# Decode block (attention times gated unit): x for the last sum by VectorE copies, and Wo's rows 0 to 30 in six pieces

## The chip, the cores and the metric

The kernel runs on one core of one Trainium2 chip, as one launch. The metric is the device time in microseconds (us). A core has a matrix engine (PE; its weight loads are listed as PEld), VectorE (DVE), ScalarE (ACT), GpSimd (POOL), SyncE (SP, which here only issues DMAs) and 16 DMA engines that move data between HBM and the on-chip memory, SBUF. Each engine works through its own list of instructions in order, and an instruction waits on semaphores for what it needs.

## The reference, cut to what matters

```
x = A_x                                  # 8 x 1 x 512, bfloat16
xn = layernorm(x)
q = xn @ wq                              # 32 heads of 128
k, v = last 2048 positions of the caches # 8 kv heads, 4 q heads share one
p = softmax(q k^T * 128 ** -0.5)
s = (p v) @ wo                           # 4096 x 512
b = (sigmoid(xn @ w_gate) * (xn @ w_up)) @ w_down
out = x + s * silu(b)
```

Everything is bfloat16 in memory. The change touches two of these terms only: the `x` of the last sum, and how `wo` gets into SBUF.

## The kernel before, in words

All large data comes through a ring of five SBUF buffers of 4 MB each (`ring_tile`). Every load is issued by SP, on one DMA queue, in a fixed order (`loads`): Wq, K of the batch rows 0 to 2, V of row 0, then K and V in turn to the last row, then w_gate and w_up (one buffer), w_down, and Wo. `issue_loads` hands out a load whenever `free_bufs` says that a buffer has come free. K and V take 4 MB for each of the 8 batch rows, 64 MB of the 81 MB that the kernel reads.

At the start VectorE computes the layer norm from `x_bf` (the loaded x), PE transposes it, and VectorE then builds a number of small constants from an identity matrix (lines 212 to 287) while POOL makes others (masks, zero fills). Those constants are used from the first softmax on. The query is projected when Wq has landed.

The loop over `b` (line 614) does, for each batch row, the turning of K on VectorE (`k_turn`, four pieces), the scores on PE (`qk`), the softmax, and the product with V of earlier rows (`pv`, `pv_rows`). The result of all rows is gathered in `o2_sb`.

After the loop come the gated unit (`unit_in`, `unit_mid`, `unit_out`, which leaves silu(b) in `gate`) and the product with Wo. `load_wo` brings the 32 row blocks of Wo (a block is 128 KB, one row `m` for each of the 128 partitions) in five DMAs for the blocks 0 to 30, then block 31 in two halves of 64 KB. `out_row(m, s)` multiplies block `m`: four matmuls for the two halves `s` and the two column parts `c`. A block's matmuls wait for the DMA that brought it. The sum over `m` of half 0 is complete, and is multiplied by `gate` into `prod` (line 690), when the first half of block 31 has gone through; the second half follows the same way. Then line 694 adds x:

```
nc.vector.tensor_tensor(out=y_bf[:], in0=prod[:], in1=x2_sb[:], op=ALU.add)
```

and SP and ACT each store one half of the columns (line 696).

In this layout column part 0 lies on the partitions 0 to 7 and part 1 on 32 to 39. So x is wanted once more, in `x2_sb`, with its first 256 columns on partitions 0 to 7 and the other 256 on 32 to 39. `x2_sb` is cleared by POOL at the start (line 94). `load_x2` fills it: POOL copies the first half from `x_bf` (line 122), and SP issues a 4 KB DMA for the second half (line 123). That load stands in the list right after V of row 1 and takes no ring buffer.

The DMAs use eight completion semaphores in turn. Before a DMA is issued, SP waits until the one that used the same semaphore last has landed. At the end of the kernel this means that each half of Wo's block 31 (line 153) is issued only when an earlier load (w_gate for the first, w_up for the second) is there.

Of the kernel before, what the change touches and what calls it, by code (L numbers as in the profile page):

```python
# [10 lines left out]
def kernel(  # L11
# [13 lines left out]
    nc = tc.nc  # L25
    P = 128
    B, _, D = A_x.shape
# [22 lines left out]
    NCOL = 2  # L50
    DC = D // NCOL
# [31 lines left out]
    x_bf = work.tile([B, D], bf16, name="x_bf")  # L83
    nc.scalar.dma_start(out=x_bf[:], in_=A_x.flatten_outer_dims())

    def ring_tile(name):
        return ring.tile([P, BIG], bf16, name=name, tag="ring", align_bytes=ALIGN)
# [5 lines left out]
    x2_sb = work.tile([NCOL * 32, DC], bf16, name="x2_sb")  # L93
# [24 lines left out]
        v_tiles[b] = t  # L118
        load_heads(t, A_v_cache, b)

    def load_x2():
        nc.gpsimd.tensor_copy(out=x2_sb[:B, :], in_=x_bf[:, :DC])
        nc.sync.dma_start(
            out=x2_sb[32 : 32 + B, :], in_=A_x.flatten_outer_dims()[:, DC:]
        )

    def load_in():
        t = ring_tile("wgu_sb")
        for n, w in enumerate((B_w_gate, B_w_up)):
            v = t[:, n * KT * F : (n + 1) * KT * F].rearrange(  # L130
                "p (kt n) -> p kt n", kt=KT
            )
            nc.sync.dma_start(out=v, in_=w.rearrange("(p kt) n -> p kt n", kt=KT))
            w_tiles["gu"[n]] = v
# [7 lines left out]
    def load_wo():  # L142
        t = ring_tile("wo_sb")
        v = t[:].rearrange("p (m n) -> p m n", m=MR)
        src = A_wo.rearrange("(p m) n -> p m n", m=MR)
        for m0, m1 in ((0, 11), (11, 19), (19, 25), (25, 29), (29, 31)):
            nc.sync.dma_start(out=v[:, m0:m1, :], in_=src[:, m0:m1, :])  # L147
        last, last_src = (
            w[:, MR - 1, :].rearrange("p (c s n) -> p s c n", c=NCOL, s=2)
            for w in (v, src)  # L150
        )
        for s in range(2):
            nc.sync.dma_start(out=last[:, s], in_=last_src[:, s])
        w_tiles["o"] = v

    loads = [(load_wq,), (load_k, 0), (load_k, 1), (load_k, 2), (load_v, 0)]
    for b in range(3, B):
        loads += [(load_k, b), (load_v, b - 2)]
        if b == 3:
            loads.append((load_x2,))  # L160
    loads += [(load_v, B - 2), (load_v, B - 1), (load_in,), (load_down,), (load_wo,)]
    free_bufs = [RING]

    def issue_loads():
        while loads:
            small_one = loads[0][0] is load_x2
            if not small_one and free_bufs[0] == 0:
                return
            f, *a = loads.pop(0)
            f(*a)  # L170
            if not small_one:
                free_bufs[0] -= 1

    issue_loads()


# [14 lines left out]
        out=rstd[:], in_=mv[:, 1:2], func=AF.Sqrt, bias=eps_t[:], scale=1.0  # L191
# [4 lines left out]
        out=xn_bf[:],  # L196
# [7 lines left out]
    for kt in range(KT):  # L204
        nc.tensor.transpose(
            out=xnT_ps[:, kt, :], in_=xn_bf[:B, kt::KT], identity=ident[:B, :B]
        )
    xnT_sb = work.tile([P, KT, PW], bf16, name="xnT_sb")
    nc.vector.memzero(xnT_sb[:])
    nc.vector.tensor_copy(out=xnT_sb[:, :, :B], in_=xnT_ps[:])  # L210

    rows16 = consts.tile([P, GR], f32, name="rows16")
    nc.vector.tensor_reduce(
        out=rows16[:],
        in_=ident[:].rearrange("p (g x) -> p x g", x=GR),
# [4 lines left out]
    for gg in range(NG):  # L220
# [3 lines left out]
            out=t[:, :, gg],  # L224
            in_=rows16[:]
# [8 lines left out]
        out=quarter[:],  # L234
        in_=ident[:].rearrange("p (h q) -> p q h", q=QP),
# [4 lines left out]
        out=block[:], in_=quarter[:].unsqueeze(2).to_broadcast([P, QP, PW])  # L240
# [3 lines left out]
        out=same[:],  # L244
        in_=ident[:].rearrange("p (g j r) -> p g r j", j=QP, r=rep),
# [5 lines left out]
        out=SumM[:].rearrange("p (g j r) -> p g j r", j=QP, r=rep),  # L251
        in_=same[:]
# [6 lines left out]
        out=Jneg[:],  # L259
        in_=ident[:].rearrange("p (a j r) -> p j a r", j=QP, r=rep),  # L260
# [4 lines left out]
        out=Jneg[:], in0=Jneg[:], scalar1=-scale, scalar2=None, op0=ALU.mult  # L265
# [3 lines left out]
        out=Hm[:],  # L269
        in_=ident[:].rearrange("p (a gl) -> p gl a", gl=GL),  # L270
# [5 lines left out]
        out=Cm4[:],  # L276
        in_=ident[:].rearrange("p (u c x) -> p c u x", c=4, x=GR),
# [5 lines left out]
        out=Cm2[:],  # L283
        in_=ident[:].rearrange("p (u c x) -> p c u x", c=2, x=GR),
# [5 lines left out]
        out=heads[:], in_=same[:].unsqueeze(2).to_broadcast([P, XR, QP])  # L290
# [3 lines left out]
        out=spr[:],  # L294
        in_=ident[:].rearrange("k (gl cl p) -> k cl p gl", gl=GL, cl=CL),
    )
    quad = consts.tile([P, QP, QP, PW], bf16, name="quad")
    for a in range(QP):
        nc.gpsimd.tensor_copy(
            out=quad[:, :, a, :], in_=ident[:].rearrange("k (a w) -> k a w", a=QP)  # L300
# [10 lines left out]
    for s in range(2):  # L311
# [13 lines left out]
        for e in range(2):  # L325
            nc.vector.tensor_copy(  # L326
                out=qx_sb[:, s, :, :, e, :],
                in_=q_ps[:].rearrange(
                    "p (r wb w e) -> p e r wb w", r=rep, wb=WE // 2, e=2
                )[:, e],  # L330
            )
    free_bufs[0] += 1
    issue_loads()
    qT_sb = work.tile([P, 2 * rep * WE, PW], bf16, name="qT_sb")
    nc.vector.transpose(
        out=qT_sb[:].rearrange("p m b -> p (m b)"),
        in_=qx_sb[:].rearrange("p s r wb e w -> p (s r wb e w)"),
    )
    qc_sb = work.tile([P, GL, NG, rep, WE, B], bf16, name="qc_sb")
    for i in range(2):  # L340
        qr_ps = psum.tile([P, 2, 2 * rep * WE * B], f32, name="qr_ps", tag="o_ps")
        for aa in range(2):
# [9 lines left out]
            out=qc_sb[:, 2 * i : 2 * i + 2].rearrange("p gl g r we b -> p (gl g r we b)"),  # L352
            in_=qr_ps[:].rearrange("p a m -> p (a m)"),
# [260 lines left out]
    for b in range(B + 1):  # L614
# [25 lines left out]
        if turn:  # L640
            qk(b)
            free_bufs[0] += 1
            issue_loads()
            if s - 1 >= 0:
                for gg in range(NG):
                    pv(s - 1, gg)
        else:
            pv(s - 1, 1)
# [37 lines left out]
    for m in range(MR):  # L686
        for s, n in enumerate(halves):
            out_row(m, s)
            if m == MR - 1:
                nc.vector.tensor_tensor(  # L690
                    out=prod[:, n], in0=gate[:, n], in1=a_ps[s][:], op=ALU.mult
# [3 lines left out]
    for c in range(NCOL):  # L695
        queues[c].dma_start(
            out=out.flatten_outer_dims()[:, DC * c : DC * (c + 1)],
            in_=y_bf[32 * c : 32 * c + B, :],
# [31 lines left out]
```

## Time and profile before

| What | Value |
|---|---|
| median of 3 runs | 197.61 us (197.59 to 197.65) |
| profiled execution | 197.44 us, of which the profile's span is 195.7 us |
| outside the span | 1.74 us |
| mean granted PE clock | 0.81 |
| busy: PE, DVE, ACT, POOL | 57%, 60%, 20%, 3% of the span |
| DMA queue of SP | 6368 packets, 81.01 MB, 97.2% of 16 engines' span |
| HBM read | 414 GB/s over the span |
| POOL copy into x2_sb (line 122) | 0.39 us, at 11.12 us |
| issue of the x DMA (line 123) | at 38.7 us |
| matmuls with Wo (line 676) | 128, busy 4.6 us, from 185.9 us |

All times in the profile are us from the start of the span. In the timeline a line gives the start, the time from the first to the last of a group, the engine, the source line, the operation, and in brackets the idle time before it with what ended it. In the chain of work that ended last, each line gives start, duration and what the end was waiting for. In the table by stretches, a column gives an engine's busy time with its number of instructions, and the last three are the granted PE clock, the mean busy share of the 16 DMA engines and GB/s. The profile lists the tile `x2_sb` as `x_sb` and `o2_sb` as `o_sb`.

### The profile page before, as it was taken

The numbers are of one execution on the slowest core, as the hardware profiler recorded it, in microseconds if no ns is written. First come the engines' busy times: TensorE is split into PE (matmuls) and PEld (weight loads), VectorE is DVE, ScalarE is ACT, GpSimd is POOL, SyncE is SP. The second block draws the span as 40 slices with busy tenths as digits, with TensorE's granted clock in tenths as the row PEclk, the third lists the DMA queues.
The fourth block names the chain that finished last, engine by engine and source line by source line (L and its number), as shares of the span: only waits on it lengthen the run. The fifth ranks groups of instructions, "written<-read, shape, count | busy, mean of one in ns | idle before, by whom it ended". The sixth has DMA issues, their size and how long they took to land.

```text
span 195.7 us, 2620 instructions
## 1 busy us (share of the span) xinstructions
PE 111.6 (57%) x1092; PEld 44.6 (23%) x1092; DVE 117.6 (60%) x176; ACT 38.6 (20%) x112; POOL 6.4 (3%) x22
## 2 busy tenths in 40 slices
PE   0133025709809980799059914990796199684362
PEld 0011001102002240214022411150215024462351
DVE  3404498299299449935895489739936952455001
ACT  3001910015015011501141104211501110233000
POOL 2730000000000000000000000000000000000000
PEclk9999555966985996589757985699589669999998
DMA  6999999999999999999999999999999999999991
GB/s 241 457 408 442 432 429 429 429 432 425 429 429 429 427 429 429 432 424 439 432 439 422 439 435 435 429 432 425 432 429 429 425 429 429 429 431 429 416 396 41
DMA packets 6410, 81.17 MB, mean 415 GB/s; under 512 B 992, under 2 KB 1024, under 8 KB 1408
## 3 DMA queue, kind: packets, MB, share of 16 engines
q1 hardware_dynamic: 6368, 81.01, 97.2%
q8 instruction: 8, 0.13, 0.2%
q10 hardware_dynamic: 32, 0.01, 0.0%
q14 instruction: 2, 0.02, 0.0%
HBM read 81.01 MB, written 0.01 MB: 414 GB/s over the span
## 4 chain that ended last, share of the span: by engine, by line
PE 38%; DVE 35%; DMA 23%; ACT 1%; issue 1%; SPq 1%; DVEq 0%
PE s_ps L401 27%; DVE k_sb L384 27%; DMA wo_sb<-in_A_wo_dram 12%; DMA k_sb<-in_A_k_cache_dram 11%; PE o_ps L501 8%; DVE pt_bf L441 2%; DVE o_r L522 2%; PE o_ps L530 1%; DVE o_sb L552 1%; ACT o_r L518 1%; DVE o_q L543 1%; DVE mx L414 1%; PE a_ps L676 1%; SPq L147 0%; SPq L101 0%
## 5 line engine op out<-in xcount | busy, mean ns | idle before, releaser
L384 DVE STREAM_TRANSPOSE k_sb<-k_sb 128x2048 uint32<-128x2048 uint32 x32 | 72.9, 2291 | 5.7 <-DMA k_sb<-in_A_k_cache_dram 5.7
L401 PE MATMUL s_ps<-k_sb,qz 128*32 128x512 bf16 x256 | 61.6, 1086 | 11.8 <-DVE k_sb L384 11.5
L447 PE MATMUL pc_ps<-pt_bf,spr 128*32 128x128 bf16 x128 | 4.7, 292 | 40.7 <-DVE pt_bf L441 40.7
L414 DVE TENSOR_REDUCE mx<-s_ps 128x1 f32<-128x512 f32 x8 | 5.5, 691 | 29.0 <-PE s_ps L401 29.0
L501 PE MATMUL o_ps<-v_sb,pT_sb 128*32 128x256 bf16 (+1 forms) x416 | 21.0, 298 | 0.0
L401 PEld LDWEIGHTS <-qz 128*32 128x32 bf16 x256 | 8.8, 115 | 49.8 <-issue 49.7
L501 PEld LDWEIGHTS <-pT_sb 128*32 128x32 bf16 (+1 forms) x416 | 14.0, 101 | 14.5 <-issue 9.9
L362 ACT COPY qz<-qc_sb 32x64 bf16<-32x64 bf16 x64 | 16.4, 302 | 0.7
L518 ACT ACTIVATE o_r<-o_ps,Cm 128x128 f32<-128x128 f32 x16 | 5.9, 368 | 52.0 <-PE o_ps L501 52.0
L522 DVE SCALAR_TENSOR_TENSOR o_r<-o_ps,Cm,o_r 128x128 f32<-128x128 f32 x28 | 9.7, 350 | 9.8 <-ACT o_r L518 9.3
L428 ACT ACTIVATE p_bf<-s_ps,nm 128x512 bf16<-128x512 f32 x8 | 5.5, 687 | 49.7 <-DVE nm L425 49.7
L447 PEld LDWEIGHTS <-spr 128*32 128x32 bf16 x128 | 3.4, 121 | 41.4 <-issue 40.7
L530 PE MATMUL o_ps<-o_r,rows 128*128 128x128 f32 x32 | 7.5, 320 | 4.8 <-DVE o_r L522 4.8
L483 DVE TENSOR_SCALAR pT_sb<-pc_bf,Hm 128x512 bf16<-128x512 bf16 x32 | 9.0, 352 | 0.2 <-ACT pc_bf L457 0.2
L457 ACT CAST pc_bf<-pc_ps 128x512 bf16<-128x512 f32 x8 | 4.7, 586 | 20.3 <-PE pc_ps L447 20.3
L316 PE MATMUL q_ps<-wq_sb,xnT_sb 128*32 128x512 bf16 x32 | 3.8, 626 | 6.8 <-DMA wq_sb<-in_A_wq_dram 6.5
L676 PE MATMUL a_ps<-wo_sb,o_sb 128*32 128x128 bf16 x128 | 4.6, 219 | 3.9 <-DMA wo_sb<-in_A_wo_dram 3.9
L530 PEld LDWEIGHTS o_ps<-o_r,rows 128*128 128x128 f32 x32 | 4.8, 189 | 6.7 <-DVE o_r L522 6.7
L326 DVE CAST qx_sb<-q_ps 128x256 bf16<-128x256 f32 x4 | 1.5, 420 | 7.7 <-PE q_ps L316 7.7
L441 DVE STREAM_TRANSPOSE pt_bf<-p_bf 128x512 bf16<-128x512 bf16 x8 | 5.4, 675 | 0.9 <-ACT p_bf L428 0.9
L543 DVE SCALAR_TENSOR_TENSOR o_q<-o_ps,rden,block 128x128 f32<-128x128 f32 x8 | 2.8, 351 | 4.7 <-PE o_ps L530 4.7
L690 DVE TENSOR_TENSOR prod<-gate,a_ps 64x128 bf16<-64x128 f32 x2 | 0.5, 279 | 7.5 <-PE a_ps L676 7.5
(64 smaller groups left out, 56.2 us busy)
## 6 DMA issues: line engine op xcount, KB each, us to landing
k_sb<-in_A_k_cache_dram SPq DMA_DIRECT2D x8, 4096.0 KB, 29.9
v_sb<-in_A_v_cache_dram SPq DMA_DIRECT2D x8, 4096.0 KB, 23.4
wq_sb<-in_A_wq_dram SPq DMA_DIRECT2D x1, 3072.0 KB, 11.6
wgu_sb<-in_B_w_gate_dram SPq DMA_DIRECT2D x1, 1792.0 KB, 25.1
wgu_sb<-in_B_w_up_dram SPq DMA_DIRECT2D x1, 1792.0 KB, 28.9
wd_sb<-in_B_w_down_dram SPq DMA_DIRECT2D x1, 1792.0 KB
wo_sb<-in_A_wo_dram SPq DMA_DIRECT2D x1, 1408.0 KB
wq_sb<-in_A_wq_dram SPq DMA_DIRECT2D x1, 1024.0 KB
```

The source lines that it names most:

```text
L362: nc.scalar.copy(out=z[rows, GL * gg : GL * (gg + 1), :, c0 : c0 + rep], in_=qc_sb[rows, :, gg, :, :, b].rearrange("p gl r we -> p gl we r"),)
L384: nc.vector.transpose(out=words, in_=words)
L401: nc.tensor.matmul(s_tiles[b][PW * gl : PW * (gl + 1), :], lhsT=qz[b % 2][:, h, we, :], rhs=kv[:, gg, gl, we // 2, we % 2], start=(we == 0 ...
L414: nc.vector.reduce_max(out=mx[:], in_=s_tiles[b][:], axis=AX.X)
L441: nc.vector.transpose(out=pt_bf[:].rearrange("p c g a r -> p (c g a r)"), in_=p_bf[:])
L447: nc.tensor.matmul(pc_ps[PW * a : PW * (a + 1), cl], lhsT=spr[:, cl].rearrange("k p gl -> k (p gl)"), rhs=pt_bf[:, :, :, a, :], start=True ...
L483: nc.vector.tensor_scalar(out=pT[:, :, :, gl, :], in0=pc[:].rearrange("p c g r -> p g c r"), scalar1=Hm[:, gl : gl + 1], scalar2=None, op0 ...
L501: nc.tensor.matmul(o_ps[rows * cg : rows * (cg + 1), :], lhsT=pT_tiles[b][:, gg, nch * m : nch * (m + 1)].rearrange("p c g r -> p (c g r)" ...
L518: nc.scalar.activation(out=o_r[:], in_=o_ps[:, 0:Dh], func=AF.Copy, scale=cm[:, 0:1])
L522: nc.vector.scalar_tensor_tensor(out=o_r[:], in0=o_ps[:, Dh * c : Dh * (c + 1)], scalar=cm[:, c : c + 1], in1=o_r[:], op0=ALU.mult, op1=AL ...
L530: nc.tensor.matmul(o2_ps[:], lhsT=rows128[gg][:].rearrange("p gl g r q -> p (gl g r q)"), rhs=o_r[:], start=(gg == 0), stop=(gg == NG - 1),)
L676: nc.tensor.matmul(a_ps[s][32 * c : 32 * (c + 1), :], lhsT=o2_sb[:, m, :], rhs=w_tiles["o"][:, m, DC * c + HC * s : DC * c + HC * (s + 1)] ...
```

## The change

The x for the last sum is no longer loaded a second time. `load_x2` is gone, with its POOL copy, its DMA and the exception for it in `issue_loads`. Instead VectorE makes two copies from `x_bf` into `x2_sb`, right after it has written the transposed layer norm (`xnT_sb`) and before it builds the constants. Blocks 0 to 30 of Wo come in six DMAs, of 7, 7, 6, 5, 4 and 2 blocks, where there were five, of 11, 8, 6, 4 and 2. The two halves of block 31 are as before.

```diff
-    def load_x2():
-        nc.gpsimd.tensor_copy(out=x2_sb[:B, :], in_=x_bf[:, :DC])
-        nc.sync.dma_start(
-            out=x2_sb[32 : 32 + B, :], in_=A_x.flatten_outer_dims()[:, DC:]
-        )
-
...
-        for m0, m1 in ((0, 11), (11, 19), (19, 25), (25, 29), (29, 31)):
+        for m0, m1 in ((0, 7), (7, 14), (14, 20), (20, 25), (25, 29), (29, 31)):
             nc.sync.dma_start(out=v[:, m0:m1, :], in_=src[:, m0:m1, :])
...
-        if b == 3:
-            loads.append((load_x2,))
...
     def issue_loads():
-        while loads:
-            small_one = loads[0][0] is load_x2
-            if not small_one and free_bufs[0] == 0:
-                return
+        while loads and free_bufs[0]:
             f, *a = loads.pop(0)
             f(*a)
-            if not small_one:
-                free_bufs[0] -= 1
+            free_bufs[0] -= 1
...
     nc.vector.tensor_copy(out=xnT_sb[:, :, :B], in_=xnT_ps[:])
+
+    for c in range(NCOL):
+        nc.vector.tensor_copy(
+            out=x2_sb[32 * c : 32 * c + B, :], in_=x_bf[:, DC * c : DC * (c + 1)]
+        )
```

## The prediction

> **What bounds the kernel now.** I read the page first, for which resource is full:
>
> ```profile
> DMA  6999999999999999999999999999999999999991
> q1 hardware_dynamic: 6368, 81.01, 97.2%
> q8 instruction: 8, 0.13, 0.2%
> ```
>
> The 16 DMA engines are busy in every slice but the first and the last, and SP's queue alone fills 97.2% of them. No compute engine is above 60%. So the time is the time to move 81 MB, and before and after it a short head and tail; work on other engines counts only where the transfers have not begun or are over. The second queue line will matter for a rival: eight transfers of instructions, 16 KB each.
>
> Next the chain of waits, for the tail, with one pair of VectorE instructions from the middle for comparison:
>
> ```profile
> 94.14 0.36 DVE o_q L543
> 94.50 0.02 issue
> 94.53 0.38 DVE o_sb L552
> ...
> 167.94 23.33 DMA wo_sb<-in_A_wo_dram
> ...
> 192.47 0.51 DVE prod L690 x2
> 192.98 0.03 DVEq L694
> 193.01 0.04 issue
> 193.06 0.28 DVE y_bf L694
> ```
>
> From 167.94 to 191.27 the end waits for nothing but a piece of Wo. Then come the last matmuls, the two products, the sum with x and the store. Between the second product and the sum lie 0.08 us, part of it the sequencer's own (DVEq), where o_q to o_sb, which also depend on each other, take 0.03.
>
> Then the timeline, for how Wo's pieces arrive and whether PE keeps up:
>
> ```profile
> 173.87 4.63 SPq L153 DMA_DIRECT2D wo_sb<-in_A_wo_dram  x2
> ...
> 182.43 1.71 PE L599 MATMUL b_ps<-wd_sb,hT_sb 128*32 128x256 bf16 x28 [3.33 <-DMA wd_sb<-in_B_w_down_dram]
> ...
> 185.86 1.41 PE L676 MATMUL a_ps<-wo_sb,o_sb 128*32 128x128 bf16 x44 [1.72 <-DMA wo_sb<-in_A_wo_dram]
> ...
> 188.22 1.07 PE L676 MATMUL a_ps<-wo_sb,o_sb 128*32 128x128 bf16 x32 [0.96 <-DMA wo_sb<-in_A_wo_dram]
> ...
> 190.07 0.85 PE L676 MATMUL a_ps<-wo_sb,o_sb 128*32 128x128 bf16 x24 [0.78 <-DMA wo_sb<-in_A_wo_dram]
> ...
> 191.32 1.33 PE L676 MATMUL a_ps<-wo_sb,o_sb 128*32 128x128 bf16 x28 [0.40 <-DMA wo_sb<-in_A_wo_dram]
> ```
>
> PE waits before every piece, 3.9 us in all, and has finished one before the next lands: blocks 19 to 24 are done at 190.92, and block 25 is there at 191.3. PE carries no backlog into the last pieces. The issues at L153 wait for w_gate (173.9) and w_up (178.1, the second).
>
> Last the busy share of the DMA engines in the tail, by half microseconds:
>
> ```profile
> 190.00:190.50 0.50, 0.43 (x16) 0.43 (x17) 0.00 (x0) 0.00 (x0) 0.00 (x0) 1.00 1.01 334
> 190.50:191.00 0.50, 0.42 (x16) 0.28 (x10) 0.00 (x0) 0.00 (x0) 0.00 (x0) 1.00 0.68 227
> 191.00:191.50 0.50, 0.18 (x8) 0.18 (x9) 0.00 (x0) 0.00 (x0) 0.00 (x0) 1.00 0.60 206
> 191.50:192.00 0.50, 0.49 (x18) 0.35 (x14) 0.00 (x0) 0.00 (x0) 0.00 (x0) 1.00 0.53 117
> ```
>
> The share falls from full to about a half at 190.5 and stays there until 192.0. So the engines do not end together: some have nothing left 1.5 us before the others, and a piece counts as landed when the last engine has its part. The late engines set the end.
>
> **The change part by part.**
>
> *x by VectorE.* It removes one POOL copy (0.39 us at 11.12) and one 4 KB DMA. The POOL copy was the last thing on POOL: nothing is gained. It adds two VectorE copies of 8x256. The nearest rows are the copy of the transposed norm (0.17) and the conversion of x (8x512, 0.41): 0.3 to 0.8 us together. They stand ahead of the constants, which now end at 7.6 + 0.8 = 8.4 at the latest; VectorE's next work, on the query, starts at 14.32, behind Wq's landing at 12.8. That is the cover for VectorE. POOL waits for the first of these constants (6.08) and does its other fills behind it: its last, now done at 11.2, moves to 12.0; PE wants POOL's `quad` at 18.21 and ACT wants the cleared `qz` at 19.79. Cost 0. If that cover were gone, K of row 0, awaited until 22.50, would still cover it.
>
> The issue of the x DMA at 38.7 stood between SP's V load at 38.05 and a K load at 52.98 that waited for its buffer: no load moves. In the transfers, 4 KB in eight rows are gone. At 429 GB/s over 16 engines that is 0.02 us on each of eight engines, and a fixed part of up to 0.05 (next paragraph) with it. It counts at the end only if a late engine carried it. Between 0 and 0.07; I take a gain of 0.02, nearer to the bytes since half of the engines gain nothing.
>
> The sum at L694 waited for three things: VectorE's own product, POOL and the x DMA. In the changed order it waits for VectorE alone. The gap of 0.08 should become that of o_q to o_sb, 0.03. A gain of 0.05, between 0 and 0.08.
>
> *Wo in six pieces.* The bytes are the same, and so are the last three DMAs' contents (4 blocks, 2, two halves). One DMA is added to a full queue. Its price: PE's start moves by 1.85 us (188.22 to 190.07) for six blocks and 1.25 (to 191.32) for four, so a block takes 0.30 and each DMA 0.05 besides. The first step, 2.36 for eight, would make it -0.04. I take a loss of 0.05, the value where PE was surely waiting at both ends, between -0.04 and twice that, 0.10. The issue itself (0.42 on SP, in a row from 166.62) is far ahead of the data.
>
> The Trainium skill, "DMA: Bandwidth & Descriptors", section "Anatomy of one DMA", gives each DMA a fixed cost of about 2.0 us beside its bytes, fitted on DMAs of the software path, and the section "Bandwidth" advises 1 MiB or more for each; the first pieces here go from 1408 and 1024 KB to 896. By that figure the sum would be an estimated 199.6. The trace speaks against it for queued DMAs: pieces of 768 and 512 KB came 1.85 and 1.25 us after the one before, which is no more than their bytes and 0.05.
>
> The semaphores turn one further, so three issues move. The pieces are issued behind one another as before, but the one with blocks 29 and 30 now waits for w_gate (173.9, it went at about 169.6), the first half of block 31 for w_up (178.1), the second for w_down (182.4). Behind them SP has only the store, at 193. The cover: from 182.4 on all of Wo is still to come, 32 blocks x 0.30 = 9.6 us, and a small DMA alone is there after 1.9 us (x at the start: issued 0.73, used 2.66). So it costs 0, with 7 us to spare.
>
> PE gets its first blocks at about 182.4 + 7 x 0.30 + 0.05 = 184.6, after the gated unit's matmuls (done 184.14), instead of 185.86. Then pieces of 7, 6, 5 arrive at 186.7, 188.6 and 190.1 and take PE 0.7 to 1.0 each. Block 25 comes when it came, plus 0.05. PE only waits in other places: no gain.
>
> Sum: +0.05 - 0.02 - 0.05 = -0.02. The span of 195.7 becomes 195.68, and with the 1.74 around it 197.42 for the profiled execution, which lay 0.17 under the median of the runs. On that median: 197.59. The ends of the terms give +0.10 and -0.19, so 197.42 to 197.71 for this case.
>
> **The rivals.**
>
> *Slower: an instruction transfer meets a late engine.* Queue 8's eight transfers took 0.2% of 16 x 195.7, that is 6.3 us, or 0.8 us each on one engine. Such transfers can be what sets engines behind; the uneven tail fits. One lies in the tail (between 184 and 193, one packet). If PE's moved waits bring it onto an engine that is already late, the end moves by 0.8: 198.4. It decides as soon as the engine hit is one of those still busy after 190.5. Against it: PE has the same 1092 matmuls, reaches block 19 within 0.2 us of the old time, and half of the engines have 1.5 us to spare.
>
> *Faster: the same the other way.* If one transfer set the last engine's lag and now falls elsewhere, 0.8 less: 196.8. Against it: the half that is busy to the end is several engines, which would all have to gain.
>
> *Faster: the x transfer cost its engines more than its bytes.* Around its landing (70 to 71) the DMA share is 0.75; if that quarter of a microsecond was lost, on half of the engines, it is 0.5 each: 197.1. Against it: the next microsecond shows 1.23, which makes it up.
>
> *Slower: the last half comes late.* Its DMAs took 16.3 us from issue to landing. If that were its own time, 182.4 + 16.3 = 198.7 instead of 192.4 would give 203.9. It decides from 10 us on. But the two halves were issued 4.3 us apart and used 0.2 apart, so it was the queue.
>
> *Slower: each DMA pays its lone time.* If the added DMA cost the 1.9 us of the first x load, 199.5; the steps of 1.85 and 1.25 exclude it unless the queue runs dry.
>
> **How the numbers follow.** A measurement of this kernel can tell about 0.2%, 0.4 us, from no change. The forecast, 197.59, has 0.77, and lies wholly within 0.2%. The transfer on a late engine has 0.07, a late last half 0.02, the lone time 0.02, and a cause of loss that I do not see 0.02: slower 0.13. The transfer the other way has 0.04, and the costly x 0.06: faster 0.10. The range is the forecast's own, widened by the 0.17 between profiled run and median and towards the nearest rivals: 197.3 to 197.9.
>
> **What would show it.** VectorE's two copies near 5.6, and no later start of the query or of K's first turn at 22.5. PE's four waits for Wo become five, the first ending near 184.6 and the last near 191.35. The last half is issued near 182.4, and no wait follows from it. The gap before the sum is 0.03. The prediction is wrong if the last wait for Wo ends before 191.0 or after 191.7, or if the DMA share falls at another time than 190.5 to 192.1.

## The result and the profile after

The changed kernel takes 197.92 us (median of 22 runs, 197.81 to 198.28), the kernel before 197.62 (22 runs beside them, 197.43 to 197.74). The ratio is 1.0016, with a 95% interval of 1.001 to 1.0023: slower by 0.3 us. That is less than 0.2%, but the interval excludes no change. The forecast was 197.59, its range 197.3 to 197.9. The profiled execution took 197.83 us with a span of 196.0, so 0.39 more than the one shown of before.

The page of the changed kernel shows the same bound:

```profile
DMA  6999999999999999999999999999999999999991
q1 hardware_dynamic: 6496, 81.01, 97.1%
q8 instruction: 8, 0.13, 0.2%
```

128 packets more for the same bytes, the DMA engines as full as before. The chain of waits, for the tail (start, duration, what the end waited for):

```profile
169.61 21.78 DMA wo_sb<-in_A_wo_dram
191.40 0.04 issue
191.44 0.62 PE a_ps L669 x16
192.06 0.02 issue
192.08 0.47 PE a_ps L669 x10
192.55 0.02 issue
192.58 0.50 DVE prod L683 x2
193.08 0.02 issue
193.10 0.28 DVE y_bf L687
```

The last wait for Wo ends at 191.40 instead of 191.27, the products start at 192.58 instead of 192.47. Between product and sum are now 0.02 us where there were 0.08, and no sequencer step. So the sum with x starts at 193.10, only 0.04 later than before. The timeline of SP and PE in the tail:

```profile
178.18 4.74 SPq L147 DMA_DIRECT2D wo_sb<-in_A_wo_dram  x2
...
182.57 2.74 PE L592 MATMUL b_ps<-wd_sb,hT_sb 128*32 128x256 bf16 x28 [2.66 <-DMA wd_sb<-in_B_w_down_dram]
...
185.07 2.72 PE L669 MATMUL a_ps<-wo_sb,o_sb 128*32 128x128 bf16 x56
...
188.66 0.85 PE L669 MATMUL a_ps<-wo_sb,o_sb 128*32 128x128 bf16 x24 [0.87 <-DMA wo_sb<-in_A_wo_dram]
190.19 0.73 PE L669 MATMUL a_ps<-wo_sb,o_sb 128*32 128x128 bf16 x20 [0.69 <-DMA wo_sb<-in_A_wo_dram]
191.44 1.31 PE L669 MATMUL a_ps<-wo_sb,o_sb 128*32 128x128 bf16 x28 [0.51 <-DMA wo_sb<-in_A_wo_dram]
```

The halves of block 31 are issued at 178.2 and 182.5 as the turned semaphores ask, and nothing waits for them. The DMA share by half microseconds falls where it fell before:

```profile
190.00:190.50 0.50, 0.31 (x12) 0.31 (x13) 0.00 (x0) 0.00 (x0) 0.00 (x0) 1.00 1.03 350
190.50:191.00 0.50, 0.43 (x16) 0.29 (x11) 0.00 (x0) 0.00 (x0) 0.00 (x0) 1.00 0.67 241
...
191.50:192.00 0.50, 0.50 (x16) 0.42 (x16) 0.00 (x0) 0.00 (x0) 0.00 (x0) 1.00 0.54 127
```

All of this gives 0.04 us. The store is issued at 193.37 before and 193.41 after:

```profile
193.37 0.32 SPq L696 DMA_DIRECT2D out_dram<-y_bf  x1
...
193.41 0.37 SPq L689 DMA_DIRECT2D out_dram<-y_bf  x1
```

Yet the span ends at 195.7 and 196.0, and the runs end at 197.44 and 197.83. From the store's issue to the end of the run it is 4.07 us before and 4.42 after. That is where the time went: into the end of the program, after the last computation. The chain of waits does not reach there. What shows it is the list of the sequencers' instructions under the program's closing line: duration in ns (min/median/max), then the first and the last start. Of the kernel before:

```profile
L725 DVEq DRAIN  x2: 19/158/297, 193.1 to 195.2; - x2
L725 ACTq DRAIN  x2: 8/124/240, 193.7 to 195.2; - x2
L725 ACTq EVENT_SEMAPHORE  x2: 17/17/17, 195.1 to 195.6; - x2
L725 DVEq EVENT_SEMAPHORE  x2: 21/21/21, 195.1 to 195.7; - x2
```

and of the changed one:

```profile
L718 DVEq DRAIN  x2: 121/222/322, 193.1 to 195.7; - x2
L718 ACTq DRAIN  x2: 8/122/236, 193.8 to 195.3; - x2
L718 ACTq EVENT_SEMAPHORE  x2: 17/17/17, 195.2 to 195.9; - x2
L718 DVEq EVENT_SEMAPHORE  x2: 21/21/21, 195.2 to 196.0; - x2
```

The engines meet twice at the end: each drains, waits on a semaphore, drains again, waits again. Before, VectorE's second drain comes with ScalarE's (195.2), and its last wait 0.1 after ScalarE's. In the changed kernel VectorE's second drain is 0.4 later than ScalarE's (195.7 against 195.3), and so all engines' last waits are at 195.9 to 196.0.

Counted through the trace, VectorE has 192 recorded instructions before (sequencer ones included) and 193 after: two copies more, one separate semaphore wait ahead of the sum fewer. The late instruction is the 192nd in both, and starts 0.48 us after the one before it: in the kernel before it is the very last wait, in the changed kernel the drain, which others wait for. Theory E says that this place in VectorE's list costs the time; its rival D is that the transfers do (the added piece, the moved issues).

### The profile page after: what moved, and what is told of

Read it like the earlier page. It is cut to its first block, busy times and chain, and to the rows that moved or that the text cites. A ratio compares the mean times of both kernels' runs of the same rounds, so it can differ in the third digit from the quotient of the medians.

```text
span 196.0 us, 2620 instructions
## 1 busy us (share of the span) xinstructions
PE 114.5 (58%) x1092; PEld 47.9 (24%) x1092; DVE 118.0 (60%) x178; ACT 38.6 (20%) x112; POOL 6.1 (3%) x21
## 4 chain that ended last, share of the span: by engine, by line
PE 35%; DMA 33%; DVE 28%; issue 1%; ACT 1%; SPq 0%; DVEq 0%
PE s_ps L394 25%; DVE k_sb L377 21%; DMA v_sb<-in_A_v_cache_dram 12%; DMA wo_sb<-in_A_wo_dram 11%; DMA k_sb<-in_A_k_cache_dram 11%; PE o_ps L494 6%; DVE o_r L515 2%; DVE pt_bf L434 2%; PE o_ps L523 1%; PE pc_ps L440 1%; PE den_ps L459 1%; DVE o_sb L545 1%; ACT o_r L511 1%; DVE o_q L536 1%; DVE mx L407 1%
## 5 line engine op out<-in xcount | busy, mean ns | idle before, releaser
L494 PE MATMUL o_ps<-v_sb,pT_sb 128*32 128x256 bf16 (+1 forms) x416 | 22.3, 314 | 0.0
L394 PEld LDWEIGHTS <-qz 128*32 128x32 bf16 x256 | 9.5, 115 | 49.0 <-issue 48.9
L494 PEld LDWEIGHTS <-pT_sb 128*32 128x32 bf16 (+1 forms) x416 | 14.9, 107 | 14.8 <-issue 9.8
L669 PE MATMUL a_ps<-wo_sb,o_sb 128*32 128x128 bf16 x128 | 5.5, 238 | 2.2 <-DMA wo_sb<-in_A_wo_dram 2.1
L669 PEld LDWEIGHTS <-o_sb 128*32 128x32 bf16 x128 | 4.7, 108 | 3.1 <-issue 2.9
```

The source lines that it names most:

```text
L394: nc.tensor.matmul(s_tiles[b][PW * gl : PW * (gl + 1), :], lhsT=qz[b % 2][:, h, we, :], rhs=kv[:, gg, gl, we // 2, we % 2], start=(we == 0 ...
L494: nc.tensor.matmul(o_ps[rows * cg : rows * (cg + 1), :], lhsT=pT_tiles[b][:, gg, nch * m : nch * (m + 1)].rearrange("p c g r -> p (c g r)" ...
L669: nc.tensor.matmul(a_ps[s][32 * c : 32 * (c + 1), :], lhsT=o2_sb[:, m, :], rhs=w_tiles["o"][:, m, DC * c + HC * s : DC * c + HC * (s + 1)] ...
```

## The experiments

Times are medians against the kernel before on the same chip (197.57, 197.55 and 197.59 in the three groups). "Store to end" is the profiled run's time less the start of SP's store.

| Kernel | VectorE list | us | against before | ratio, 95% interval | store to end |
|---|---|---|---|---|---|
| before | 192 | 197.62 | | | 4.07 |
| changed | 193 | 197.92 | +0.30 | 1.0016 (1.001 to 1.0023) | 4.42 |
| x_only | 193 | 197.89 | +0.32 | 1.0017 (1.0008 to 1.0026) | 4.45 |
| wo_only | 192 | 197.70 | +0.13 | 1.0008 (0.9998 to 1.0018) | 4.17 |
| before_p1 | 193 | 197.85 | +0.28 | 1.001 (1.0 to 1.0019) | 4.39 |
| after_m1 | 192 | 197.63 | +0.06 | 1.0 (0.9992 to 1.0009) | 4.09 |
| after_p2 | 195 | 197.67 | +0.12 | 1.001 (1.0001 to 1.0019) | 4.11 |
| after_p3 | 196 | 197.60 | +0.05 | 1.0005 (0.9997 to 1.0014) | 4.09 |
| before_m1 | 191 | 197.72 | +0.17 | 1.0012 (1.0003 to 1.0021) | 4.21 |
| x_only_m2 | 191 | 197.67 | +0.12 | 1.0005 (0.9996 to 1.0014) | 4.27 |
| before_p2 | 194 | 197.59 | 0.00 | 0.9999 (0.999 to 1.0008) | 4.07 |
| before_p65 | 257 | 197.55 | -0.04 | 0.9997 (0.9988 to 1.0006) | 4.11 |
| x_only_p2 | 195 | 197.66 | +0.07 | 1.0006 (0.9997 to 1.0016) | 4.15 |
| wo_15 | 192 | 198.67 | +1.08 | 1.0051 (1.0038 to 1.0064) | 4.26 |

The intervals are about 0.1% (0.2 us) to each side, so differences of 0.1 between two kernels are not told apart by the times; the column of the traces is sharper. The ratio, which is not that of the medians, is even the same 1.001 for before_p1 and after_p2; their traces differ (4.39 against 4.11).

Part of the spread in the last column is the store's own time: 1.75 to 1.93 us from its issue until VectorE's first closing wait is over. From there to the end of the run it is 2.31 to 2.36 us in every kernel with a list of 192 or of 194 and more, 2.62 to 2.64 in the three with 193, and 2.45 in the two with 191.

### One part alone, and one VectorE instruction more or fewer

x_only, from the changed kernel:

```diff
-        for m0, m1 in ((0, 7), (7, 14), (14, 20), (20, 25), (25, 29), (29, 31)):
+        for m0, m1 in ((0, 11), (11, 19), (19, 25), (25, 29), (29, 31)):
```

> The x copies alone (Wo in the old five pieces). Theory E, the end of VectorE's list: in both traces the 192nd recorded VectorE instruction comes late; in the kernel before it is the very last one, a semaphore wait after the closing barrier (195.72, where the other engines have theirs at 195.6), in the changed kernel, which has one VectorE instruction more in all, it is the drain ahead of it (195.67 instead of about 195.28), and the barrier waits for it. This kernel has the same VectorE list as the changed one, so it should have most of the loss: 197.75 to 197.9, about 0.05 below the changed kernel, the closing part from the store's issue to the end of the span 2.6 us as in the changed kernel (2.37 before). Rival D, the transfers: the added piece and the moved issues cost the time; then this kernel gains from the shorter gap before the sum and comes at 197.55 to 197.6.

wo_only is the opposite edit, made to the kernel before.

> Wo in six pieces alone, x as before. Theory E: VectorE's list is that of the kernel before, the end is not touched, and only the added DMA shows: 0.05 to 0.1 slower, 197.67 to 197.72, closing part 2.37 us. Rival D: the whole loss, 197.9.

before_p1, from the kernel before:

```diff
+    for n in range(1):
+        pad = consts.tile([P, 1], f32, name=f"pad{n}")
+        nc.vector.memset(pad[:], 0.0)
     heads = consts.tile([P, XR, QP], f32, name="heads")
```

> The kernel before with one VectorE instruction more: a fill of an unused column of 128 values, put among the constants, where VectorE has six microseconds to spare. Theory E: the late 192nd instruction becomes the drain, as in the changed kernel: 197.85 to 197.95, closing part 2.6 us. Rival D, and every other theory that I have: no change, 197.62.

after_m1, from the changed kernel:

```diff
-    nc.vector.memset(eps_t[:], 1e-5)
+    nc.gpsimd.memset(eps_t[:], 1e-5)
```

> The changed kernel with one VectorE instruction fewer: the fill of eps goes to POOL. The VectorE list is then as long as that of the kernel before. Theory E: 197.6 to 197.68, closing part 2.37 us. Rival D: 197.9, as the changed kernel.

All four went as theory E says. The x copies alone have the whole loss, the six pieces alone have 0.13 with an interval that includes no change. One fill of an unused column, where VectorE is idle, costs 0.28 by the medians, with an interval of the ratio that begins at 1.0; one fill fewer in the changed kernel takes its +0.30 down to +0.06. The closing lines of before_p1:

```profile
L728 DVEq DRAIN  x2: 137/217/297, 193.1 to 195.6; - x2
L728 ACTq DRAIN  x2: 8/124/241, 193.7 to 195.2; - x2
L728 ACTq EVENT_SEMAPHORE  x2: 17/17/17, 195.1 to 195.9; - x2
```

Again VectorE's drain comes 0.4 after ScalarE's, with a sum that starts where it did (193.05). In x_only, wo_only, before_p1 and after_m1 the 192nd instruction starts 0.48 us after the one before it, as in the first two traces. So it is the one instruction more in VectorE's list, not the copies' work and not the transfers, that costs most of the 0.3. Rival D falls as the cause.

### Where else the 192nd may stand

after_p2 and after_p3 add two and three such fills to the changed kernel. before_m1 gives the fill of eps to POOL in the kernel before. x_only_m2 does that in x_only, and gives the clearing of `xnT_sb` to POOL too.

> The changed kernel with two VectorE instructions more (fills of unused columns among the constants). If the late instruction is the 192nd from the start, whatever it is, it is now the drain right after the sum with x, which has 1.7 us to spare because the store is still on its way. Theory E: nothing of the lateness is left, closing part 2.25 us, time 197.5 to 197.6, so faster than the changed kernel by 0.3 to 0.4 though it does more. If instead a longer VectorE list costs in itself: 198.0 or more.

> The changed kernel with three VectorE instructions more. By theory E the 192nd is now the sum with x itself. The late instruction started 0.48 us after the one before it in every trace so far; the second product starts at about 192.79 and the sum normally at 193.10, so the sum should start at about 193.27, 0.17 late, on the path to the end, with the closing part clean at 2.25 us: 197.68 to 197.75, between the kernel with two more and the changed one. If the count does not matter from two on: 197.55, as with two.

> The kernel before with one VectorE instruction fewer (eps filled by POOL), so that its list has 191. Theory E: there is no 192nd instruction, the last wait of VectorE comes with those of the other engines, 0.12 earlier: 197.45 to 197.52, closing part 2.25 us. If the lateness goes with the last instruction and not with the 192nd: 197.57 to 197.62, as before.

> x by VectorE, Wo in the old five pieces, and two of VectorE's small fills (eps and the cleared transposed norm) given to POOL: 191 VectorE instructions. Theory E: no late end (0.12 less than before), the gap before the sum shorter by 0.05, no added DMA: 197.40 to 197.47, the fastest of all. Rival D: 197.55.

The first came near (0.07 above its range): with two instructions more the changed kernel is 0.18 faster relative to the kernel before than without them, and store to end is 4.11. VectorE's drain is with the others again:

```profile
L721 DVEq DRAIN  x2: 19/170/322, 193.4 to 195.5; - x2
L721 ACTq DRAIN  x2: 8/122/236, 194.0 to 195.5; - x2
```

The other three missed, and they trim theory E. In after_p3 the 192nd is the sum with x, and it is not late: it starts 0.31 after the second product, as in the changed kernel. In after_p2 the 192nd, the drain behind the sum, is not late either. So in these lists the place costs only where it is one of the last two. And a list of 191, which has no 192nd instruction, gains nothing. Its last waits are in step with the others':

```profile
L725 ACTq EVENT_SEMAPHORE  x2: 17/17/17, 195.2 to 195.6; - x2
L725 DVEq EVENT_SEMAPHORE  x2: 21/21/21, 195.2 to 195.6; - x2
```

but what lies outside the span is 1.93 us in before_m1 and x_only_m2, against 1.70 in the kernel before (the 1.74 of the table before is from a rounded span). By the spans listed to 0.1 us it is 1.88 to 1.98 in all 22 runs of the two, and 1.64 to 1.79 in the 32 of the kernel before beside them. It is as if the late place had moved out of what the profile records; the transfers of instructions in the next part point that way, but both kernels also have the longest GpSimd list (39 recorded instructions), and no run separates the two.

### Two more, many more, and the best of the parts

before_p2 and before_p65 add 2 and 65 fills to the kernel before, x_only_p2 adds two to x_only.

> The kernel before with two VectorE instructions more, 194 in all; the 192nd is then the wait of the closing barrier, whose answer comes 2 us after the drain ahead of it. If only the last two places of the list are harmful, the part from the store's issue to the end of the profiled run (4.07 us before, 4.39 with one more) is back at about 4.1 and the time at 197.5 to 197.65. If any longer list is slower: 197.85, as with one.

> The kernel before with 65 VectorE instructions more, 257 in all, all of them in VectorE's free time before the query. If the late place recurs every 64 instructions, the 256th is the closing drain and the loss of the kernel with one more is back: 197.8 to 197.9, store to end 4.39. If it is that one place, or a larger block, nothing is late: 197.5 to 197.65, store to end 4.1.

> A candidate for the fastest: x by VectorE, Wo in the old five pieces, and two fills more so that VectorE has 195 instructions and none of the last two is the 192nd. The shorter gap before the sum stays (0.05), the loss at the end is gone: 197.45 to 197.6, that is 0 to 0.1 below the kernel before; with the changed kernel's theory of a costly transfer (rival D) the same. If a VectorE copy of x costs in itself: over 197.65.

With 194 and with 257 instructions nothing is lost: 0.00 and -0.04. So the loss is no price of length, and does not come back every 64 instructions.

The trace of before_p65 has a second late place, though, and with it shows what the two are. Its 64th VectorE instruction is one of the fills. It starts 0.43 us after the one before it, where the fills ahead of it come less than 0.05 us apart, and it has nothing to wait for:

```profile
8.05 0.60 DVE L290 MEMSET pad<- 128x1 f32 x43
9.02 0.65 DVE L290 MEMSET pad<- 128x1 f32 x22 [0.37 <-issue]
```

DMA queue 14 carries transfers of instructions, 8 KB each. From the start of the span on, the kernel before has three, at 66.7, 84.6 and 196.4 us (the last behind the span's end), and before_p65 has three, at 12.1, 85.0 and 126.6. The first and the last go with VectorE's list, the middle one does not. In the seven kernels where the 192nd is one of the last two, the last transfer starts 0.67 to 0.84 us after that instruction. In the lists of 194 and more it starts ahead of the 192nd: at 194.9 in before_p2, at 188.7 to 189.1 in after_p2, after_p3 and x_only_p2, where VectorE waits for the last matmuls. With 191 it starts at 196.8 and 196.9, 1.15 us after the last recorded wait. So the late places, 128 instructions apart, go with the refilling of VectorE's instructions, and nothing is late where the refill begins ahead of the place.

x_only_p2, with the x copies and no late place, was expected at 0 to 0.1 below the kernel before and is at +0.07, its interval on both sides of 1: the shorter gap before the sum brings nothing that these runs can show. None of the twelve is faster than the kernel before beyond its interval.

### The price of one DMA

wo_15, from the kernel before:

```diff
-        for m0, m1 in ((0, 11), (11, 19), (19, 25), (25, 29), (29, 31)):
+        for m0, m1 in ((0, 2), (2, 4), (4, 6), (6, 8), (8, 10), (10, 12), (12, 14), (14, 16), (16, 18), (18, 20), (20, 22), (22, 24), (24, 25), (25, 29), (29, 31)):
```

> The price of a DMA, by ten more: x as before, blocks 0 to 24 of Wo in twelve pairs and a single, then 4 and 2 and the two halves, so 15 DMAs where there were five. At 0.05 each, as the prediction took it: 0.5 more, 198.05. At 0.10, the prediction's upper end: 198.55. At the 1.9 us of a lone DMA: 216.

It is slower by 1.08, 0.11 for each added DMA, just over the prediction's upper end of 0.10. The trace splits that. Its timeline and the stretches (busy time of PE, PEld, DVE, ACT and POOL, then the granted PE clock, DMA share, GB/s):

```profile
191.81 1.68 PE L676 MATMUL a_ps<-wo_sb,o_sb 128*32 128x128 bf16 x28 [0.97 <-DMA wo_sb<-in_A_wo_dram]
```

```profile
191.00:192.00 1.00, 0.19 (x5) 0.19 (x6) 0.00 (x0) 0.00 (x0) 0.00 (x0) 0.57 0.61 206
192.00:193.00 1.00, 1.00 (x24) 1.00 (x22) 0.00 (x0) 0.00 (x0) 0.00 (x0) 0.50 0.21 45
```

The last wait for Wo ends at 191.81 instead of 191.32, and the last landing is at 192.85 instead of 192.38 by the trace's completions: 0.47 to 0.49 for ten DMAs, so 0.05 each. The rest came behind it: PE ran at a granted clock of 0.50, was busy without a gap to the end, and the first product started at 193.42, 0.57 after the last landing, where it was 0.09 before, and the store took 1.93 us until VectorE's first closing wait was over, where it was 1.76. All five runs of wo_15 lie between 198.47 and 198.83; whether the clock was low in all of them is not shown.

## Why the prediction was wrong, by its own steps

**The bound and the tail.** Right. The transfers set the time, the last wait for Wo ended at 191.40 and the DMA share fell at 190.5, both inside the limits that the prediction set for itself. PE waited for Wo's pieces without a backlog at the end; it showed three such waits and not five, since at a granted clock of 0.50 to 0.76 (184 to 187 us; 1.00 before) it worked through the first two pieces in one go (56 matmuls in 2.72 us). That cost nothing, as block 25 was awaited all the same.

**x by VectorE, the work.** Right: the two copies (0.43 us from 5.60) shifted the constants and POOL's fills by 0.5, and VectorE still stood idle for 6.2 us before the query.

**x by VectorE, the list.** This is the step that failed. The prediction said "Cost 0" for the two copies and added "the 1.74 around it" and all that follows the store as a constant. It counted the work that the instructions do and the waits that they change, but not that VectorE's list becomes one instruction longer, and what then stands where in the closing part. The runs put 0.28 on one such instruction (before_p1), and the changed kernel's trace has 0.35 more from store to end (4.42 against 4.07). What stands there is the closing drain, late as the 192nd, at a refill of VectorE's instructions. No row of the page or of the chain of waits showed this place; the sequencers' closing rows of the kernel before did show VectorE's last wait 0.1 behind the other engines'.

**The gap before the sum.** Right in size in the trace: 0.08 became 0.02. In the times it cannot be seen: x_only_p2, which has it and no late place, is at +0.07.

**The x transfer.** A gain of 0.02 was taken; nothing in the runs resolves it.

**One DMA more.** The 0.05 was right for the transfers, shown with ten of them (0.47). The changed kernel's own profile has 0.11 to 0.13 there, and single profiles differ by as much: wo_only's last landing, with the same DMA more, was 0.04 earlier than that of before. The Trainium skill's fixed 2.0 us for a DMA ("DMA: Bandwidth & Descriptors", "Anatomy of one DMA") does not apply to DMAs queued behind others here: ten more would have cost an estimated 20 us, and cost 1.08.

**The moved issues.** Right: the last half went out at 182.5, 0.02 behind the landing of w_down, and no wait followed.

**The rivals.** None of them is what happened. The eight instruction transfers of queue 8 came at nearly the same places (177.5 and 188.3 us for the last two, 177.3 and 189.5 before), and the last one still hit an engine with time to spare: in both traces one of the seven that landed first fell back, and the last engine's lag did not grow. The price of 0.8 for such a hit was too low, since in the kernel before the first of these transfers set an engine about 1.3 us behind the others. One argument against this rival was misread: block 19, said to be reached within 0.2 us of the old time (190.07), was done at 189.51; it is block 20 that started at 190.19. The sum of what the traces show, +0.05 to 0.12 for the DMA, -0.06 for the gap and +0.35 for the end, is 0.34 to 0.41, against 0.39 between the two profiled runs and 0.30 between the medians. The range missed by 0.02 us because it gave the unseen cause of loss a chance of 0.02 and no room.

What stays open is what VectorE's sequencer does at that place for 0.4 us. The instruction does not wait for the bytes, since the transfer starts only after it. The Trainium skill, "Runtime: NRT & Kernel Launch", section "Instruction fetch mechanics", says that engines' instructions are refilled in 16 KiB blocks of 256 and that crossing a boundary is mostly hidden. The traces agree with the block for queue 8 (eight transfers of 16 KB, while PE has 2194 recorded instructions with its weight loads) and differ for VectorE: 8 KB, and places 128 apart. They agree that it is mostly hidden: the 64th instruction is late in before_p65 alone. The 0.48 us in the closing part were not hidden.

## What to carry to other kernels

An instruction that does nothing on any path can still move the time through its place in its engine's list. When a change of a few tenths of a microsecond is at stake, compare the sequencers' closing instructions of all engines, and the time from the last store to the end of the run, before any of it is put down to the edit's work. Adding and removing one idle instruction tells such an effect from the edit's own: here that test costs one line, and it separated 0.24 (after_m1) to 0.28 us (before_p1) of the 0.30. A transfer of instructions that moves when one idle instruction is added shows where such a place lies.

## What was not expected of the hardware

- VectorE's 192nd recorded instruction starts 0.48 us after the one before it in every trace where it is one of its last two (seven kernels, 0.477 to 0.482). It starts without delay where it is the drain behind the sum or the sum itself. A list of 194, 195, 196 or 257 instructions ends in step with the other engines. An 8 KB transfer of instructions on queue 14 goes with this place and with the 64th.
- The instruction transfers of 16 KB on queue 8 (PE's, to judge by their number and places) take 0.88 to 1.02 us each and set one DMA engine behind for good. In the kernel before, the first three loads of K land on all 16 engines within 0.45 us; after the transfer at 48.0 us the next load lands 1.65 us after its first engine on its last, and the last half of Wo is spread over 1.61 us: six engines within 0.29 us, two at 0.76 to 0.77, eight at 1.40 to 1.61. Each transfer on queue 8 adds one engine to the late group, each of the two 8 KB transfers one to the middle group. This is the uneven tail, and a load counts as landed by its slowest engine.
- The granted PE clock in the tail differs between executions of near-equal programs, and can put PE on the path, as in wo_15. In x_only's profile PE was granted 0.50 for a time and had no gap from 188.50 on, yet the first product started 0.09 us after the last landing, as before, so nothing was lost:

```profile
188.50 3.74 PE a_ps L669 x72
```

```profile
190.00:191.00 1.00, 1.00 (x22) 0.85 (x19) 0.00 (x0) 0.00 (x0) 0.00 (x0) 0.50 0.81 276
```
